# A two-stage FFT convolution with a soft mixture of experts: a first stage in tiles of 60 and 30 columns, x loaded two chunks at a time, and the last 26 rows of z loaded through GpSimd

## The chip, the cores and the metric

The kernel runs on one core of a Trainium2 chip. The metric is the device time of one execution in microseconds (us), the median of several runs. All data are float32. Engines are named as in the profile: PE is TensorE (PEld its weight loads), DVE is VectorE, ACT is ScalarE, POOL is GpSimd, SP is SyncE, which here only issues transfers.

## The reference

A causal long convolution of 8 sequences of 5696 tokens by 128 channels with one filter per channel, then a soft mixture of experts over all 45568 tokens: each of 32 slots (8 experts of 4) takes a softmax over tokens, each token a softmax over slots.

```python
# convolution: x (8, 5696, 128), h (5696, 128)
L = 2 * S
y = irfft(rfft(x, n=L, axis=1) * rfft(h, n=L, axis=0)[None], n=L, axis=1)[:, :S, :]
x = y.reshape(B * S, D)
# soft mixture of experts: phi (128, 32), w1 (8, 128, 1024), w2 (8, 1024, 128)
logits = x @ phi
d = softmax over tokens of logits          # columns
slot_input = (d.T @ x).reshape(E, 4, D)
slot_out[e] = maximum(slot_input[e] @ w1[e], 0) @ w2[e]
c = softmax over slots of logits           # rows
out = c @ slot_out
```

## The kernel before

The transform is split in two steps, 5696 = 89 x 64 with 90 frequencies in the first factor (`N1`) and 64 in the second (`N2`). Only half of a symmetric pair of columns is computed: a fold (sum and difference of a column and its mirror) halves the work. The filter h counts as group 0, the 8 sequences as groups 1 to 8. Each group has 8 chunks of 4 columns and their 4 mirrors; a chunk is one step `t` of the main loop.

- **First stage** (`load_x`, `fold`, `stage_a`). `load_x(c)` loads a chunk with its mirror columns into one of three buffers `xc`, in two DMAs on SP (80 rows and 9 rows, pieces of 2 KB). `fold` (L202, POOL) writes the sum (comp 0) or the difference (comp 1) into `x`. `stage_a(c, comp)` multiplies it by two 128-wide tables `s1` (L213: 128 rows, 128 columns, 512 moved), which hold the 90 frequencies in two blocks of 45 columns; ACT copies each bank to `fst` (L215), and two DMAs on SP store it in the DRAM scratch `f` (L219) in pieces of 1 KB. A fp32 product shows as two matmul records in the profile.
- **Second stage** (`load_g`, `stage_b1`, `stage_b2`), in units of 4 frequencies (the 12th unit of a group has 1). `gt` is loaded from `f` on SP (128 partitions, 4 KB each; L237), multiplied by `wt` (L251, 64x64 quarters) into the two-bank PSUM tile `bt`; DVE multiplies by the filter's spectrum (L269, L278) into `yf`; `stage_b2` transforms back with `vt` (L293) into the two-bank tile `bz`, ACT copies it to `zst` (L298), and SP stores it in the scratch `z` (L301).
- **Third stage** (`load_pair`, `stage_c1` to `stage_c6`), in pairs of chunks. `load_pair(T)` brings z into the one buffer `zc`: 64 of the 90 rows to partitions 32 to 95, and 26 rows in four DMAs of 8, 8, 8 and 2 rows to every fourth partition of 0 to 31 (`z_blocks`), 16 KB a row, all on SP (L329). `stage_c1` multiplies by `i1` (L348, two halves of 64 columns in one bank); ACT and DVE undo the fold (L353 to L361), and its second part `after` makes four sums on POOL (L367) that give the tokens `y`. Then come the transposes of y (c2, L376), the logits (c3, L385), the row maxima and exponentials (c4, L414 to L430; c5, L437; `softmax`, L445 to L450), the slot sums (`dispatch`, L461) and the token weights, kept in the scratch `c_t` (c6, L485).
- **Tail.** After the last first and second stages, the remaining five pairs of the third stage run by themselves with a second z buffer `zd`, whose unused rows are copied from `zc` as zeros (L656); then the experts (L761 to L791) and the output stage (L806 to L833), which writes 23 MB.

The order of the work is written out by hand: each engine, and each queue of DMA issues, runs its instructions in program order, and an instruction that waits holds up those behind it. The main loop (L561 to L645) runs step t: the z load of the coming pair, prefetch of `gt` for the next step, `load_x(t + 3)`, `stage_a(t, 0)`, `fold(t + 1, 0)`, dispatch, a second-stage unit, the third stage's products (every other step), transposes, a second-stage unit, `stage_a(t, 1)`, `fold(t + 1, 1)`, logits, and the rest. First-stage steps are t = 0 to 71, second-stage units t = 9 to 80, third-stage products start at t = 27. A step has one or two units of the second stage in turn.

Four PSUM banks (`bank()`) are shared in turn by all stages but the second, which has its own two two-bank tiles, `bt` and `bz`.

Of the kernel before, what the change touches and what calls it, by code (L numbers as in the profile page):

```python
# [17 lines left out]
def z_blocks(n):  # L18

    left = [(64 + 8 * j, min(8, n - 64 - 8 * j), j, 4) for j in range((n - 57) // 8)]  # L20
    return [(0, 64, 32, 1)] + left


def transform_tables(S, N1, N2, CH, X0, F0, F1):
# [20 lines left out]
    NP = N1 // 2  # L45
    part = s1
    s1 = np.zeros((P, 3, P))
    for a, p in enumerate((F0, F1)):
        s1[X0:X0 + R1, :, p:p + NP] = part[:, :, a * NP:(a + 1) * NP]
# [26 lines left out]
def kernel(  # L76
# [44 lines left out]
    X0, F0, F1 = 20, 6, 82  # L121
# [4 lines left out]
        for n, t in zip(("s1", "i1", "w", "v", "turn"), transform_tables(S, N1, N2, CH, X0, F0, F1))]  # L126
    fd = [nc.dram_tensor(f"f_{g}", (2, N2, NP, 2, D), F32, kind="Internal").ap() for g in range(B + 1)]
# [34 lines left out]
    s1 = apool.tile([P, 3, P], F32, name="s1", tag="s1", bufs=1)  # L162
# [12 lines left out]
    xf = [apool.tile([P, CH, D], F32, name=f"x{i}", tag=f"x{i}", bufs=1) for i in range(2)]  # L175
    xcs = [apool.tile([P, 2, CH, D], F32, name=f"xc{i}", tag=f"xc{i}", bufs=1) for i in range(3)]
# [3 lines left out]
    def load_x(c):  # L180
        if c >= (B + 1) * NJ:
            return
        g, j = divmod(c, NJ)
        src = (h if g == 0 else x[g - 1]).rearrange("(a n) d -> a n d", n=N2)
        t_ = xcs[c % len(xcs)]
        gap = N2 - CH * (2 * j + 1)
        for r in (slice(0, SPLIT), slice(SPLIT, R1)):
            v = src[r, CH * j:CH * (j + 1), :]
            v = bass.AP(tensor=v.tensor, offset=v.offset,
                        ap=[v.ap[0], [gap * D, 2], [1, CH * D]])  # L190
            nc.sync.dma_start(
                out=t_[X0 + r.start:X0 + r.stop, :, :, :].rearrange("p s n d -> p s (n d)"), in_=v)
        xs[c] = t_
# [3 lines left out]
    def fold(c, comp):  # L197
# [3 lines left out]
        y_ = xf[comp]  # L201
        nc.gpsimd.tensor_tensor(out=y_[:, :, :], in0=t_[:, 0, :, :], in1=t_[:, 1, ::-1, :],  # L202
# [3 lines left out]
    def stage_a(c, comp):  # L206
        g, j = divmod(c, NJ)
        src = folded.pop((c, comp))
        tab = (0, 1) if comp == 0 else (1, 2)
        st = apool.tile([P, CH, 2, D], F32, name="fst", tag="fst", bufs=5)  # L210
        for G in range(2):
            p = bank()
            nc.tensor.matmul(p[:, :], s1[:, tab[G], :],  # L213
                             src[:, :, :].rearrange("p n d -> p (n d)"), start=True, stop=True)
            nc.scalar.activation(st[:, :, G, :],  # L215
                                 p[:, :].rearrange("p (n d) -> p n d", d=D), AF.Copy)
        n0 = comp * HALF + CH * j
        for a, p in enumerate((F0, F1)):
            nc.sync.dma_start(  # L219
                out=fd[g][a, n0:n0 + CH, :, :, :].rearrange("n q c d -> q n (c d)"),  # L220
                in_=st[p:p + NP, :, :, :].rearrange("k n c d -> k n (c d)"))


# [7 lines left out]
    def load_g(u):  # L231
        if u >= (B + 1) * NW:
# [3 lines left out]
        t_ = bpool.tile([P, 4, 2, D], F32, name="gt", tag="gt", bufs=3)  # L236
        nc.sync.dma_start(  # L237
            out=t_[:, 0:n, :, :].rearrange("p q c d -> p (q c d)"),
            in_=fd[g].rearrange("a r q c d -> (a r) (q c d)")[:, 8 * w * D:(8 * w + 2 * n) * D])
        gs[u] = t_  # L240

    def stage_b1(u, share):
        g, w, us = parts(u)
        t_ = gs.pop(u)
        tag = "bz" if g == 0 and w % 2 else "bt"
# [15 lines left out]
        pi = bpool.tile([P, 4, 2, D], F32, name="p", tag="pi", bufs=2)  # L261
# [20 lines left out]
    def stage_b2(u):  # L282
# [5 lines left out]
        bz = bps.tile([P, 2, 2, 2 * D], F32, name="bz", tag="bz")  # L288
        for o, (i, n) in enumerate(us):
            for q in range(n):  # L290
                r = slice(q * HP, (q + 1) * HP)
                for a in range(2):
                    nc.tensor.matmul(bz[a * HP:(a + 1) * HP, q, o, :], vt[r, i, a, :],  # L293
# [4 lines left out]
        nc.scalar.activation(st[:, 0:m, 0:n, :].rearrange("p o q x -> p q o x"),  # L298
                             bz[:, 0:n, 0:m, :], AF.Copy)
# [8 lines left out]
    zn = used = None  # L308
# [12 lines left out]
    def load_pair(T):  # L321
# [3 lines left out]
        t_ = zring.pop(0)  # L325
        zring.append(t_)
        w_ = 2 * 2 * CH * 2 * D
        for r, n, p, step in z_blocks(N1):
            nc.sync.dma_start(  # L329
# [3 lines left out]
        zs[T] = t_  # L333

    def stage_c1(T, between):
        t_ = zs.pop(T)
        kr = used if t_ is zn else P
# [7 lines left out]
        def product(o, tab, q):  # L345
            p = bank()
            for h_ in range(2):
                nc.tensor.matmul(p[h_ * HP:(h_ + 1) * HP, :], i1[0:kr, tab, :],  # L348
                                 t_[0:kr, h_, o, :, q, :], start=True, stop=True)
# [200 lines left out]
    for c in range(1, 3):  # L550
        load_x(c)
# [7 lines left out]
    wait_b2 = []  # L559

    for t in range(last_front + 1):  # L561
# [12 lines left out]
        turns = {2: (1, 3), 1: (2,)}.get(len(us), ())  # L574

        def slot_b(place=None):
            if place is not None and place not in turns:
                return
# [8 lines left out]
        if pair(-1) is not None:  # L587
            load_pair(pair(-1))
        if t % NJ:
            prefetch(t + 1)  # L590
        if t < NA:
            load_x(t + 3)
            stage_a(t, 0)
            fold(t + 1, 0)
        if pair(3) is not None:
            dispatch(pair(3))
        if t < last_front:
            slot_b(1)
        T, U = pair(0), pair(2)
        if t == last_front:  # L600
            assert T is None and U is None
            slot_b()
# [9 lines left out]
        rows = (lambda: None) if U is None else (lambda: stage_c4(U))  # L612
        after = None
        if T is not None:
            after = stage_c1(T, rows)
        else:
            rows()
# [245 lines left out]
```

## Time and profile before

| | us |
|---|---|
| median of 3 runs (lowest, highest) | 899.32 (898.45, 901.66) |
| the profiled execution's own time | 901.4 |
| its span, first to last instruction | 899.6 |
| PE busy in the span | 808.7 (90%) |
| DVE busy | 645.0 (72%) |
| ACT busy | 480.9 (53%) |
| POOL busy | 405.8 (45%) |
| first-stage matmuls L213, 576 records | 274.6 |
| third-stage products L348, 480 records | 117.7 |
| folds L202 on POOL, 144 of 1276 ns | 183.6 |
| evacuations L215, 288 of 597 ns | 171.8 |
| evacuations L298, 96 of 972 ns | 93.3 |

The core moved 272.44 MB by DMA (mean 303 GB/s), nearly all issued by SP; nothing was issued by POOL. The packets of that queue took 90.1% of the span of the 16 DMA engines.

How to read it: a matmul's end is modelled in the profile, so a PE that is busy is not PE at its peak, and matmuls that run side by side on different columns of the array share their time. Durations are those of single instructions on their engine; the DMA share is the mean busy share of the 16 DMA engines. The chain of waits follows the work that ended last back to its beginning, and names at each step what released it.

### The profile page before, as it was taken

Reading aid. Unit: us, or ns where it says so; the run is one execution under the profiler, and the core shown is the slowest. Engines: PE = TensorE matmul, PEld = TensorE weight load, DVE = VectorE, ACT = ScalarE, POOL = GpSimd, SP = SyncE. Lnnn points to the kernel's source line nnn. Section 1 sums busy time; section 2 is a strip of 40 time slices with the busy share of each in tenths; the row PEclk is TensorE's granted clock in tenths of the full one; section 3 lists DMA queues with packets and bytes.
Section 4 is the critical chain, followed back from the end, with each engine's and each line's share of the span. In section 5 each row is a group of like instructions: output and inputs, shape, how many; then the busy total and the mean of one; then the engine's idle time right before and its main releaser. Section 6 shows DMA issues by size and latency. Waiting matters only on the chain.

```text
span 899.6 us, 19379 instructions
## 1 busy us (share of the span) xinstructions
PE 808.7 (90%) x7220; PEld 424.0 (47%) x7220; DVE 645.0 (72%) x928; ACT 480.9 (53%) x888; POOL 405.8 (45%) x385
## 2 busy tenths in 40 slices
PE   6969888799999999999999999999988777978893
PEld 2323344344445544455555445444444444444793
DVE  3049776668778888888888777888867886873542
ACT  3624445456655566665566666666644434673441
POOL 4624323345555555555555555555533343681000
PEclk9979999999999999999999999999988999987855
DMA  9989999999999999999999999999985887770898
GB/s 297 279 262 330 301 322 333 313 333 334 308 312 335 325 309 314 330 320 316 328 319 311 318 334 321 302 330 316 320 284 202 302 281 263 270 294 2 307 405 330
DMA packets 156967, 272.44 MB, mean 303 GB/s; under 512 B 12182, under 2 KB 114838, under 8 KB 153733
## 3 DMA queue, kind: packets, MB, share of 16 engines
q1 hardware_dynamic: 156299, 270.85, 90.1%
q8 instruction: 58, 0.95, 0.4%
q10 hardware_dynamic: 576, 0.36, 0.2%
q14 instruction: 34, 0.28, 0.1%
HBM read 142.86 MB, written 128.21 MB: 301 GB/s over the span
## 4 chain that ended last, share of the span: by engine, by line
PE 71%; DMA 18%; DVE 3%; issue 3%; ACT 2%; SPq 1%; POOL 0%; DVEq 0%; ACTq 0%
PE bank L213 24%; PE bank L348 12%; PE bt L251 10%; PE bz L293 8%; DMA gt<-f 5%; DMA out_dram<-o 5%; PE bank L376 5%; PE bank L461 3%; DMA zc<-z 3%; PE bank L385 2%; PE bank L437 2%; PE bank L414 2%; DMA xc<-in_x_dram 2%; DMA f<-fst 1%; PE bank L485 1%
## 5 line engine op out<-in xcount | busy, mean ns | idle before, releaser
L202 POOL TENSOR_TENSOR x<-xc 128x512 f32<-128x512 f32 x144 | 183.6, 1276 | 237.8 <-PE bank L213 188.4
L213 PE MATMUL bank<-x,s 128*128 128x512 f32 x576 | 274.6, 613 | 8.6 <-DMA xc<-in_h_dram 8.2
L215 ACT ACTIVATE fst<-bank 128x512 f32<-128x512 f32 x288 | 171.8, 597 | 91.4 <-PE bank L213 82.1
L298 ACT ACTIVATE zst<-bz 128x1024 f32<-128x1024 f32 x96 | 93.3, 972 | 196.0 <-PE bz L293 187.8
L269 DVE TENSOR_TENSOR p<-bt,Hi 128x1024 f32<-128x1024 f32 x96 | 113.0, 1177 | 105.0 <-PE bt L251 104.5
L213 PEld LDWEIGHTS bank<-x,s 128*128 128x128 f32 x576 | 102.2, 192 | 126.0 <-issue 95.6
L251 PE MATMUL bt<-gt,wt 64*64 64x256 f32 x1620 | 117.1, 396 | 37.5 <-DMA gt<-f 17.3
L348 PE MATMUL bank<-zc,i 128*64 128x512 f32 x480 | 117.7, 613 | 6.0 <-DMA zc<-z 4.3
L278 DVE TENSOR_TENSOR yf<-bt,p 128x512 f32<-128x512 f32 x192 | 119.4, 663 | 3.3
L269 DVE TENSOR_TENSOR bt<-bt,Hr 128x1024 f32<-128x1024 f32 x96 | 113.1, 1178 | 0.0
L251 PEld LDWEIGHTS bt<-gt,wt 64*64 64x64 f32 x1620 | 55.5, 134 | 114.1 <-issue 57.7
L293 PE MATMUL bz<-yf,vt 64*64 64x256 f32 x1440 | 104.7, 388 | 0.0
L367 POOL TENSOR_TENSOR y<-y,op 128x512 f32<-128x512 f32 x64 | 77.5, 1211 | 7.6 <-DVE op L353 4.9
L293 PEld LDWEIGHTS bz<-yf,vt 64*64 64x64 f32 x1440 | 61.7, 137 | 22.1 <-issue 0.9
L367 POOL TENSOR_TENSOR y<-y,om 128x512 f32<-128x512 f32 x54 | 64.0, 1185 | 2.1
L348 PEld LDWEIGHTS bank<-zc,i 128*64 128x64 f32 x480 | 30.1, 138 | 67.2 <-issue 46.4
L422 POOL MEMSET dt<- 64x8 f32 x32 | 3.4, 107 | 124.0 <-issue 65.4
L376 PE MATMUL bank<-ident,y 109*128 109x109 f32 x512 | 57.4, 267 | 0.7 <-DVE y L367 0.7
L376 PEld LDWEIGHTS bank<-ident,y 109*128 109x128 f32 x512 | 51.0, 146 | 13.5 <-POOL L L450 6.9
L378 ACT ACTIVATE yt<-bank 128x360 f32<-128x360 f32 x128 | 50.0, 481 | 0.9 <-PE bank L376 0.9
L816 PE MATMUL op<-so,cT 32*128 32x128 f32 x704 | 45.7, 382 | 5.2 <-ACT o L825 4.8
L269 DVE TENSOR_TENSOR p<-bt,turn 128x1024 f32<-128x1024 f32 (+1 forms) x12 | 14.1, 1173 | 49.9 <-PE bt L251 49.9
(97 smaller groups left out, 858.4 us busy)
## 6 DMA issues: line engine op xcount, KB each, us to landing
f<-fst SPq DMA_DIRECT2D x288, 180.0 KB
gt<-f SPq DMA_DIRECT2D x99, 512.0 KB
z<-zst SPq DMA_DIRECT2D x88, 512.0 KB
zc<-z SPq DMA_DIRECT2D x30, 1024.0 KB
xc<-in_x_dram SPq DMA_DIRECT2D x64, 320.0 KB
out_dram<-o SPq DMA_DIRECT2D x16, 1024.0 KB
zc<-z SPq DMA_DIRECT2D x90, 128.0 KB
out_dram<-o SPq DMA_DIRECT2D x8, 768.0 KB
```

The costliest lines, as they stand in the source:

```text
L202: nc.gpsimd.tensor_tensor(out=y_[:, :, :], in0=t_[:, 0, :, :], in1=t_[:, 1, ::-1, :], op=AL.subtract if comp else AL.add)
L213: nc.tensor.matmul(p[:, :], s1[:, tab[G], :], src[:, :, :].rearrange("p n d -> p (n d)"), start=True, stop=True)
L215: nc.scalar.activation(st[:, :, G, :], p[:, :].rearrange("p (n d) -> p n d", d=D), AF.Copy)
L251: nc.tensor.matmul(bt[q * HP:(q + 1) * HP, a, o, :], wt[r, 2 * i + q, :], t_[r, 2 * o + q, :, :].rearrange("p c d -> p (c d)"), start=True ...
L269: nc.vector.tensor_tensor(out=p_, in0=pv, in1=h_, op=AL.mult)
L278: eng.tensor_tensor(out=y_[r, 0:k, c, :], in0=pv[:, :, c, :], in1=pi[r, 0:k, 1 - c, :], op=op_)
L293: nc.tensor.matmul(bz[a * HP:(a + 1) * HP, q, o, :], vt[r, i, a, :], y_[r, a * m + o, :, :].rearrange("p c d -> p (c d)"), start=True, sto ...
L298: nc.scalar.activation(st[:, 0:m, 0:n, :].rearrange("p o q x -> p q o x"), bz[:, 0:n, 0:m, :], AF.Copy)
L348: nc.tensor.matmul(p[h_ * HP:(h_ + 1) * HP, :], i1[0:kr, tab, :], t_[0:kr, h_, o, :, q, :], start=True, stop=True)
L367: eng.tensor_tensor(out=part_, in0=part(v, 0), in1=o_[:, :, :], op=sign)
L376: nc.tensor.transpose(p[:, i * TR:(i + 1) * TR], ys[T][0:TR, k * CH + i, 0:D], ident[0:TR, 0:TR])
L378: nc.scalar.activation(yt[:, k * CH:(k + 1) * CH, :, :], of_tokens(p), AF.Copy)
```

## The change

The first stage's columns are regrouped. The 90 frequencies are interleaved, and the tables `s1` hold the first 60 in one 64-wide block and the last 30 in one 32-wide block. `first_low(c)` multiplies the sum and the difference of one chunk by the 64-wide block, two products into the two halves of one bank; `first_high(c)`, every second step, multiplies the sums and differences of two chunks by the 32-wide block, four products into the four quarters of one bank. The scratch `f` is laid out frequency by frequency, so that a partition's piece is stored as 4 KB and read back, by `load_g`, in pieces of 1 KB.

`load_x` loads two chunks at once (pieces of 4 KB) into one of two larger buffers, four steps ahead, on even steps alone. Both folds of a step are made together, into four buffers.

The 26 last rows of z come in four pieces of 8, 8, 5 and 5 rows, to every fourth partition of 0 to 31 and of 96 to 127 in turn, and these four DMAs are issued by POOL; the 64 rows remain SP's. In the tail the copy of zero rows becomes six copies, and the products on `zd` take 128 rows where they took 96.

The second stage's products use two two-bank tiles, `bt0` and `bt1`, in turn; its results go through the shared banks, one evacuation per bank. Buffer counts change (`gt` 3 to 4, `p` 2 to 1, `fst` 5 to 4). The loop's order is rewritten as two strings, one for odd steps (`ORDER_E`) and one for even steps (`ORDER_O`), in which the third stage's products stand on odd steps.

```diff
 def z_blocks(n):
-    left = [(64 + 8 * j, min(8, n - 64 - 8 * j), j, 4) for j in range((n - 57) // 8)]
+    left, r, j = [], 64, 0
+    while r < n:
+        m = min(8, (n - r + 1) // 2)
+        left += [(r, m, j, 4), (r + m, min(m, n - r - m), 96 + j, 4)]
+        r, j = r + 2 * m, j + 1
     return [(0, 64, 32, 1)] + left
...
-    fd = [nc.dram_tensor(f"f_{g}", (2, N2, NP, 2, D), F32, kind="Internal").ap() for g in range(B + 1)]
+    fd = [nc.dram_tensor(f"f_{g}", (NP, 2, N2, 2, D), F32, kind="Internal").ap() for g in range(B + 1)]
...
-    xf = [apool.tile([P, CH, D], F32, name=f"x{i}", tag=f"x{i}", bufs=1) for i in range(2)]
-    xcs = [apool.tile([P, 2, CH, D], F32, name=f"xc{i}", tag=f"xc{i}", bufs=1) for i in range(3)]
+    xf = [apool.tile([P, CH, D], F32, name=f"x{i}", tag=f"x{i}", bufs=1) for i in range(4)]
+    xcs = [apool.tile([P, 2, 2 * CH, D], F32, name=f"xc{i}", tag=f"xc{i}", bufs=1) for i in range(2)]
...
     def load_x(c):
-        if c >= (B + 1) * NJ:
+        if c % 2 or c >= (B + 1) * NJ:
             return
...
             v = bass.AP(tensor=v.tensor, offset=v.offset,
-                        ap=[v.ap[0], [gap * D, 2], [1, CH * D]])
+                        ap=[v.ap[0], [gap * D, 2], [1, 2 * CH * D]])
...
-    def stage_a(c, comp):
...
+    def first_stage(tiles, width):
+        st = apool.tile([P, CH, 2, D], F32, name="fst", tag="fst", bufs=4)
         for G in range(2):
             p = bank()
-            nc.tensor.matmul(p[:, :], s1[:, tab[G], :],
-                             src[:, :, :].rearrange("p n d -> p (n d)"), start=True, stop=True)
+            for o, (c, comp) in enumerate(tiles):
+                k = slice(0, HP) if width == HP else slice(HP, HP + QP)
+                nc.tensor.matmul(p[o * width:(o + 1) * width, :], s1[:, comp + G, k],
+                                 folded[(c, comp)][:, :, :].rearrange("p n d -> p (n d)"),
+                                 start=True, stop=True)
             nc.scalar.activation(st[:, :, G, :],
                                  p[:, :].rearrange("p (n d) -> p n d", d=D), AF.Copy)
+        for o, (c, comp) in enumerate(tiles):
+            g, j = divmod(c, NJ)
+            n0 = comp * HALF + CH * j
+            k0, n = (0, N1A) if width == HP else (N1A, N1 - N1A)
             nc.sync.dma_start(
+                out=fd[g].rearrange("q a r c d -> (q a) (r c d)")[k0:k0 + n, n0 * 2 * D:(n0 + CH) * 2 * D],
+                in_=st[o * width:o * width + n, :, :, :].rearrange("k n c d -> k (n c d)"))
+
+    def first_low(c):
+        first_stage([(c, comp) for comp in range(2)], HP)
+
+    def first_high(c):
+        both = [(c - 1 + i, comp) for i in range(2) for comp in range(2)]
+        first_stage(both, QP)
...
     def load_g(u):
...
-            out=t_[:, 0:n, :, :].rearrange("p q c d -> p (q c d)"),
-            in_=fd[g].rearrange("a r q c d -> (a r) (q c d)")[:, 8 * w * D:(8 * w + 2 * n) * D])
+            out=t_[:, 0:n, :, :].rearrange("p q c d -> p q (c d)"),
+            in_=fd[g][4 * w:4 * w + n, :, :, :, :].rearrange("q a r c d -> (a r) q (c d)"))
...
-        tag = "bz" if g == 0 and w % 2 else "bt"
+        tag = f"bt{u % 2}"
...
-        bz = bps.tile([P, 2, 2, 2 * D], F32, name="bz", tag="bz")
+        bz = [bank() for _ in range(us[0][1])]
...
-        nc.scalar.activation(st[:, 0:m, 0:n, :].rearrange("p o q x -> p q o x"),
-                             bz[:, 0:n, 0:m, :], AF.Copy)
+        for q in range(n):
+            nc.scalar.activation(st[:, 0:m, q, :],
+                                 bz[q][:, 0:m * 2 * D].rearrange("p (o x) -> p o x", o=m), AF.Copy)
...
-    def load_pair(T):
+    def load_pair(T, rest=None):
...
-        for r, n, p, step in z_blocks(N1):
-            nc.sync.dma_start(
+        for i_, (r, n, p, step) in enumerate(z_blocks(N1)):
+            if rest is not None and rest != (i_ > 0):
+                continue
+            (nc.gpsimd if i_ else nc.sync).dma_start(
...
+    ORDER_E, ORDER_O, XAHEAD = "XYf1wbV5s", "Xfz2b63dxPmb", 4
...
+        work_ = {
+            "z": lambda: load_pair(pair(-1), False) if pair(-1) is not None else None,
...
+            "V": lambda: load_pair(pair(-2), True) if pair(-2) is not None else None,
...
+            "x": lambda: load_x(t + XAHEAD) if t < NA else None,
...
+            "P": lambda: prefetch(t + 2),
...
+            "X": lambda: first_low(t) if t < NA else None,
+            "Y": lambda: first_high(t) if t < NA and t % 2 else None,
+            "f": lambda: [fold(t + 1, comp) for comp in range(2)] if t < NA else None,
+            "d": lambda: dispatch(pair(3)) if pair(3) is not None else None,
+            "b": lambda: slot_b(),
+            "1": lambda: after.append(stage_c1(T, lambda: stage_c4(U) if U is not None else None))
+            if T is not None else stage_c4(U) if U is not None else None,
+            "w": lambda: [a_() for a_ in after],
+            "2": lambda: stage_c2(pair(1)) if pair(1) is not None else None,
+            "6": lambda: stage_c6(pair(5)) if pair(5) is not None else None,
+            "5": lambda: stage_c5(U) if U is not None else None,
+            "3": lambda: stage_c3(pair(1)) if pair(1) is not None else None,
+            "m": lambda: column_max(pair(1)) if pair(1) is not None else None,
+            "s": lambda: softmax(U) if U is not None else None,
...
+        for c_ in (ORDER_E if t % 2 else ORDER_O):
+            work_[c_]()
...
-    held = slice(N1 // 64 * 8 + 3, used - 64, 4)
+    held = [slice(p + k + 4 * (n if k == 0 else 0), p - p % 32 + 32, 4)
+            for _, n, p, _ in z_blocks(N1)[3:] for k in range(3)]
...
-    nc.sync.dma_start(out=zn[held, :, :, :, :, :].rearrange("k h o n c d -> k (h o n c d)"),
-                      in_=zring[0][held, :, :, :, :, :].rearrange("k h o n c d -> k (h o n c d)"))
+    for v in held:
+        nc.sync.dma_start(out=zn[v, :, :, :, :, :].rearrange("k h o n c d -> k (h o n c d)"),
+                          in_=zring[0][v, :, :, :, :, :].rearrange("k h o n c d -> k (h o n c d)"))
```

## The prediction

> **What bounds the kernel now.** I began with the page's slices, to see whether one limit holds throughout.
>
> ```profile
> PE   6969888799999999999999999999988777978893
> ...
> DMA  9989999999999999999999999999985887770898
> GB/s 297 279 262 330 301 322 333 313 333 334 308 312 335 325 309 314 330 320 316 328 319 311 318 334 321 302 330 316 320 284 202 302 281 263 270 294 2 307 405 330
> ```
>
> One slice is 22.5 us. TensorE and the DMA engines both read 9 from the 8th to the 29th slice, so shares can't say which of them leads. Busy times by stretch come next (a line: start:end and length, then busy us and instructions of each engine, granted clock, DMA share, GB/s).
>
> ```profile
> 36.00:124.00 88.00, 72.87 (x432) 31.27 (x430) 56.87 (x65) 35.22 (x57) 35.02 (x28) 0.94 0.96 296
> 124.00:178.00 54.00, 44.23 (x352) 22.01 (x352) 36.24 (x42) 25.99 (x38) 16.53 (x13) 1.00 1.00 327
> ...
> 272.10:444.80 172.70, 172.70 (x1525) 86.09 (x1525) 141.51 (x203) 106.39 (x195) 96.90 (x90) 1.00 0.98 322
> ```
>
> Until 178 us (the fill, no third stage yet) TensorE has gaps (44 of 54 us busy) and the DMA engines have none: transfers bound it. From there to about 660 us (the steady stretch) TensorE has no gap, at a granted clock of 1.00, while the DMA share is 0.98. The chain of waits decides between them (start, us, what); this is one period, two chunks, 272.09 to 293.69 = 21.60 us:
>
> ```profile
> 272.09 3.44 PE bank L213 x8
> 275.52 1.03 PE bank L461 x32
> 276.55 1.02 PE bt L251 x16
> 277.57 0.86 PE bz L293 x16
> 278.44 1.64 PE bank L376 x16
> ...
> 280.54 1.81 PE bank L213 x4
> 282.35 0.74 PE bank L385 x8
> ...
> 284.98 1.92 PE bank L213 x4
> 286.90 1.87 PE bank L348 x8
> 288.76 0.59 PE bank L414 x4
> ...
> 293.69 3.44 PE bank L213 x8
> ```
>
> Only matmuls stand on it, and periods repeat at 21.60. So the steady stretch is TensorE's by the chain, with transfers close behind. 45 chunks of third-stage steps (27 to 71) make 22.5 such periods.
>
> **First stage.** A period now spends 3.44 + 1.81 + 1.92 = 7.17 us on 16 records of L213: 0.43 us per record of 512 columns (3.44 / 8). An fp32 product leaves two records. The change makes of a chunk's four 128-wide products two pairs 64 wide and, per two chunks, two fours 32 wide. Pairs of 64 are in the trace: L348's eight records last 1.87 us, four slots of 0.43 and 0.15 more, so two run side by side. Fours of 32 are L385's: 8 records of 360 columns in 0.74 us, two slots, so four run side by side. New: two low parts at 1.87 = 3.74; one high part of four slots, between 4 x 0.43 = 1.72 and L385's row scaled, 0.74 x 2 x 512/360 = 2.10. I take 1.85 (L385's excess over its slots, 0.74 - 2 x 0.30 = 0.14, added once). 3.74 + 1.85 = 5.59; saved 1.58 (1.33 to 1.71). Period: 20.02.
>
> **ScalarE and VectorE.** The first stage loses 2 evacuations of 0.597 per period; L298's 0.974 becomes two of 0.597, at 2.8 units: -1.19 + 0.62 = -0.57 us. ScalarE has 106.4 busy of 172.7, so this is nothing on the path. VectorE keeps its work, 141.5 / 8 = 17.7 us; in 20 us it is 88% busy, still covered. The second "bt" tile lets a new second-stage product start before VectorE has finished the last. Four shared banks now also take the second-stage results; each is refilled at least four fills later, with some 0.6 us of evacuation each: nothing.
>
> **The order.** After the last third-stage product TensorE now runs second stage 1.88, L437 0.59, first stage 1.87, then the transposes L376. Their input needs GpSimd's four sums:
>
> ```profile
> 353.20 1.94 PE L348 MATMUL bank<-zc,i 128*64 128x512 f32 x8
> ...
> 355.21 1.05 POOL L430 TENSOR_TENSOR L<-L,rm 128x512 f32<-128x512 f32 x1 [0.59 <-DVE rm L429]
> ...
> 356.21 2.45 POOL L367 TENSOR_TENSOR y<-y,op 128x512 f32<-128x512 f32 x2
> ```
>
> The products end at 355.14; the sums begin at 356.21 and take 2 x 2.45, ending 5.97 us after. The last quarter of L376 would start after 1.88 + 0.59 + 1.87 + 0.75 x 1.64 = 5.57: a stall of 0.40. Period: 20.42.
>
> **z on GpSimd.** Today all five pieces are SP's:
>
> ```profile
> L329 SPq DMA_DIRECT2D zc<-z x40: 544/602/1124, 275.4 to 427.8; - x40
> ```
>
> (min/median/max ns of one issue). Four of five move to GpSimd, behind the four sums and ahead of L450 (1.05) and of the next two folds (2 x 1.28, L202), and the next first stage waits for both folds. The products that read the old z ended 5.97 us before, so that wait costs nothing. Once in four periods the last piece also waits for the last z unit, whose result leaves PSUM some 4 us before; landings on the chain of waits took 3.9 to 4.2 us (f, at 38 to 47 us). I book 0, and up to 3 us in each of 5.6 such periods, 17 in all, for the range. From a period's start: 1.87 + 1.85 + 1.87 + 0.59 + 1.87 = 8.05, then 5.97, then 4s, 1.05 and 2.56: **17.63 + 4s**, s being one issue. No row shows a GpSimd issue. Below, 0.35 (SP's shortest for gt, 347 ns); above, 1.28, GpSimd's own longest common instruction. I take 0.60, the same transfer on SP: 20.0, just under 20.42. At 0.70 this chain takes over; at 1.28 it is 22.75. If the cover goes, the folds are late, then the first stage, then everything.
>
> The Trainium skill (DMA: Bandwidth & Descriptors, Specifications) puts the first byte at about 1 us from GpSimd and 0.6 from SP. No row here shows a GpSimd issue; if that difference were all GpSimd's own time, s would be an estimated 1.0 and the period 21.6, the gain gone.
>
> **Transfers.** Bytes stay: 322 GB/s x 21.6 us = 6.96 MB a period. First-stage results are written in 4 KB pieces instead of 1 KB and read back in 1 KB instead of 4 KB: one trades for the other. x comes in 4 KB instead of 2 KB, in two DMAs a period instead of four; SP loses 6 of some 24 issues, and SP isn't bound. x's load now waits for the second chunk's fold, with the gt loads queued behind it on SP; these have half a period or more before use. A period of 20.42 needs 341 GB/s. Bounds: 327 GB/s (124 to 178 us, share 1.00) gives 21.3 us; the output's 405 GB/s gives 17.2. I take the best slice of mixed traffic, 335: **20.78 us**, 0.82 saved, x 22.5 = **18.5 us**.
>
> On the z pieces the same page (Rules for kernel authors) speaks against the change: two transfers to disjoint partition halves share the same engines, and issuing from more queues gives no bandwidth. Another section (Why a DMA increments its semaphore by 16) has an SP transfer of 8 rows run on the lowest 8 engines, and GpSimd's start from a moving cursor, which would even the load. No row here splits the share by engine; by the first rule the period stays at 20.8 to 21.3, by the second TensorE's 20.4 is reached.
>
> **Fill and tail.** The fill (36 to 178 us) moves the same bytes at full DMA share; slices 4 to 8 spread from 301 to 333 GB/s, 5% about their middle, so I book 0, between -7 and +7 us. At the tail's start the one copy of zero rows becomes six: five more issues at 0.6, 3 us at most; 1 taken. A contraction over 128 rows instead of 96 changes no row (L348: 604 against 613 ns).
>
> **Sum.** Span 899.6 - 18.5 + 0 + 1 = 882.1; the profiled execution took 901.4, 1.8 around its span, so 883.9; it lies 2.1 above the median, 899.3, which becomes **881.8, say 882**.
>
> **Rivals.**
> *TensorE's rate is reached* (25%): the even z load and longer x bursts give 341 GB/s. For: the 405 GB/s. Against: no mixed slice above 335. 22.5 x 1.18 = 26.6, fill up to -7: 867 to 874; with the shortest high part (1.71 saved), 864.
> *Transfers take the bound* (17%): 327 GB/s holds, perhaps less as 1 KB reads replace 4 KB. For: share 1.00 at that rate. Against: the evener z. 22.5 x 0.3 = 6.8: 893; with the fill's +7, 900.
> *GpSimd's issue, the slower side* (14%): 17.63 + 4s passes 21.60 at s = 0.99. For: its in-order queue stands between third stage and next first stage. Against: 602 ns for the same issue on SP. At 1.28 it is 22.75: 22.5 x 1.15 = +26: 926; at 1.1, 910.
> *Fours of 32 don't run side by side* (2%): the high part then costs 3.4 and the gain is gone, about 900; L385's row speaks against.
> *The forecast* has 42%; its own range is 874 to 891, the fill's 7 us and the tail's 1 to 2 to either side.
>
> About 0.5%, 4.5 us, is what a measurement of this kernel can tell from no change. Faster by more: the forecast, the first rival and half of the second, 0.42 + 0.25 + 0.08 = 0.75. Within: most of the rest of the second and the fours, 0.09. Slower: 0.16, GpSimd and the second's worst end. The range reaches from below the first rival's middle, with a good fill, 860, to the mild end of the slow side, 904.
>
> **What would show it.** L213's busy time per period falls from 7.2 to 5.6 and its records come in fours; the chain's period reads 20.4 to 20.9. GpSimd issues at or under 0.7 us, and no first-stage matmul waits for L202. GB/s of 335 or more in the steady stretch; about 330 to 178 us. Wrong if the chain there names GpSimd or DMA, or if gt's landings stand on it past 200 us.

## The result, and the profile after

| | before | after |
|---|---|---|
| median (lowest to highest of 4 runs each, side by side), us | 900.49 (898.45 to 902.51) | 950.87 (949.67 to 956.66) |
| ratio, 95% interval | | 1.0572 (1.0521 to 1.0623) |
| span of the profiled execution, us | 899.6 | 947.9 |

The change makes the kernel slower by 5.7%. The forecast was 882 us, its range 860 to 904: wrong in sign.

The page of after, second part (40 slices, now of 23.7 us): most slices move less than before.

```profile
DMA  8888789999999999999999999999988886863698
GB/s 269 251 259 254 212 235 331 291 320 330 299 291 300 314 295 300 318 310 308 304 308 305 297 291 294 313 304 318 308 283 281 289 304 229 282 227 126 243 406 342
```

The same three stretches as in the prediction, after:

```profile
36.00:124.00 88.00, 59.15 (x396) 18.51 (x392) 42.22 (x48) 23.20 (x39) 34.46 (x28) 0.86 0.83 245
124.00:178.00 54.00, 38.24 (x400) 15.68 (x395) 33.93 (x37) 19.37 (x35) 14.80 (x12) 0.95 0.95 285
272.10:444.80 172.70, 158.54 (x1583) 74.35 (x1580) 126.56 (x192) 94.19 (x195) 109.56 (x119) 0.98 0.99 307
```

In the first stretch of the fill the DMA share has dropped from 0.96 to 0.83: something now keeps transfers from being issued. (The granted clock is lower there too, 0.86 against 0.94; TensorE is busy for 59 of the 88 us, and no run separates the clock's part.) In the steady stretch TensorE, which had no gap in 172.7 us, idles 14.

To split the loss by stage I take the first product of the third stage as the end of the fill. The view of the tile zc gives the first and last start of these products, before and then after:

```profile
L348 PE MATMUL bank<-zc,i x480: 592/592/1112, 179.0 to 792.1; 128*64 128x512 f32 x160
```

```profile
L374 PE MATMUL bank<-zc,i x480: 592/592/1061, 207.7 to 844.4; 128*64 128x512 f32 x160
```

The products of the pair 22 periods later start at 650.5 and 700.1. So the fill loses 28.7 us, the 22 periods 20.9 (471.5 to 492.4; 21.43 to 22.38 each), and the rest, 249.1 and 247.8, gains 1.3, which is less than this part differs among the runs below (241 to 255). Sum 48.3, the difference of the spans.

What one of these periods waits for stands in the timeline of after (start, us, engine, line; in brackets the idle time before):

```profile
489.29 2.52 POOL L212 TENSOR_TENSOR x<-xc 128x512 f32<-128x512 f32 x2
...
491.84 3.09 SPq L200 DMA_DIRECT2D xc<-in_x_dram  x2
...
494.98 2.29 SPq L259 DMA_DIRECT2D gt<-f  x3
...
499.73 1.94 PE L374 MATMUL bank<-zc,i 128*64 128x512 f32 x8
...
503.67 1.09 PE L273 MATMUL bt<-gt,wt 64*64 64x256 f32 x16 [2.00 <-DMA gt<-f]
```

Read it from below. TensorE is done with the third stage's products at 501.67 and waits 2.00 us for gt. SP issued that gt only at 494.98, because the x burst is ahead of it: its buffer came free with the fold's end at 491.81, and its two DMAs took SP 3.09 us. Then gt took 8.65 us to land (494.98 to 503.62 on the chain of waits). The next period has the same wait, 2.03 us. The view of TensorE's waits in the 22 periods (207.7 to 700.1 us; total, times, longest) says what they come to:

```profile
PE bt L273 <- DMA gt<-f: 36.0, 21, 2.3
PE bank L374 <- DMA zc<-z: 4.4, 7, 1.2
```

TensorE is busy for 447.4 of these 492.4 us, 20.34 a period, and 36.0 of the other 45.0 us are waits for gt.

In the fill the same place costs more:

```profile
45.41 7.21 SPq L232 DMA_DIRECT2D f<-fst  x8
...
54.12 1.73 SPq L259 DMA_DIRECT2D gt<-f  x3
...
55.94 11.23 SPq L232 DMA_DIRECT2D f<-fst  x8
...
61.07 1.98 PE L273 MATMUL bt<-gt,wt 64*64 64x256 f32 x16 [5.57 <-DMA gt<-f]
```

SP is held for 7 and 11 us by eight stores of f each, which wait for ScalarE's copies of first-stage results (L226; 34.7 us of SP's waits from 36 to 178 us are for these); x and gt stand behind them. Until its first third-stage product TensorE waits 37.5 us for gt, where before it was 15.7.

What was to be gained is there all the same, in the groups of the page of after:

```profile
L223 PE MATMUL bank<-x,s 128*32 128x512 f32 (+1 forms) x1152 | 226.8, 624 | 18.5 <-POOL x L212 17.5
...
L357 POOL DMA_DIRECT2D zc<-z x124 | 65.1, 531 | 22.8 <-DMA z<-zst 17.4
```

The first stage's busy time is 226.8 us where L213 had 274.6, and a z issue on GpSimd takes 0.53 us.

### The profile page after: what moved, and what is told of

The parts are those of the page before. It is cut to its first block, busy times and chain, and to the rows that moved or that the text cites. A ratio compares the mean times of both kernels' runs of the same rounds, so it can differ in the third digit from the quotient of the medians.

```text
span 947.9 us, 20381 instructions
## 1 busy us (share of the span) xinstructions
PE 783.2 (83%) x7796; PEld 385.6 (41%) x7796; DVE 625.7 (66%) x927; ACT 444.2 (47%) x904; POOL 469.9 (50%) x517
## 4 chain that ended last, share of the span: by engine, by line
DMA 30%; PE 26%; POOL 8%; DVE 6%; SPq 3%; issue 2%; ACT 2%; DVEq 0%; POOLq 0%; ACTq 0%
DMA gt<-f 17%; PE bank L223 5%; PE bt L273 4%; DMA out_dram<-o 4%; PE bank L315 4%; POOL y L393 3%; PE bank L402 3%; PE bank L374 3%; DMA zc<-z 3%; SPq L200 2%; POOL x L212 2%; DMA f<-fst 2%; DMA z<-zst 2%; DMA cl<-c_t 2%; DVE yf L300 1%
## 5 line engine op out<-in xcount | busy, mean ns | idle before, releaser
L223 PE MATMUL bank<-x,s 128*32 128x512 f32 (+1 forms) x1152 | 226.8, 624 | 18.5 <-POOL x L212 17.5
L321 ACT ACTIVATE zst<-bank 128x512 f32<-128x512 f32 (+1 forms) x184 | 98.6, 585 | 243.8 <-PE bank L315 226.6
L226 ACT ACTIVATE fst<-bank 128x512 f32<-128x512 f32 x216 | 127.9, 598 | 128.1 <-PE bank L223 108.8
L273 PE MATMUL bt<-gt,wt 64*64 64x256 f32 x1620 | 121.5, 410 | 73.9 <-DMA gt<-f 73.5
L315 PE MATMUL bank<-yf,vt 64*64 64x256 f32 x1440 | 104.5, 398 | 19.4 <-DVE yf L300 19.0
L223 PEld LDWEIGHTS bank<-x,s 128*32 128x32 f32 (+1 forms) x1152 | 56.2, 128 | 152.8 <-issue 79.3
L315 PEld LDWEIGHTS bank<-yf,vt 64*64 64x64 f32 x1440 | 58.0, 138 | 51.5 <-issue 30.5
L357 POOL DMA_DIRECT2D zc<-z x124 | 65.1, 531 | 22.8 <-DMA z<-zst 17.4
L402 PE MATMUL bank<-ident,y 109*128 109x109 f32 x512 | 62.3, 274 | 10.2 <-POOL y L393 9.5
L379 DVE TENSOR_TENSOR y<-bank,y 128x512 f32<-128x512 f32 x32 | 22.1, 690 | 62.9 <-PE bank L374 62.1
```

Of the source, the lines that this page charges most:

```text
L223: nc.tensor.matmul(p[o * width:(o + 1) * width, :], s1[:, comp + G, k], folded[(c, comp)][:, :, :].rearrange("p n d -> p (n d)"), start=Tr ...
L226: nc.scalar.activation(st[:, :, G, :], p[:, :].rearrange("p (n d) -> p n d", d=D), AF.Copy)
L273: nc.tensor.matmul(bt[q * HP:(q + 1) * HP, a, o, :], wt[r, 2 * i + q, :], t_[r, 2 * o + q, :, :].rearrange("p c d -> p (c d)"), start=True ...
L315: nc.tensor.matmul(bz[q][a * HP:(a + 1) * HP, o * 2 * D:(o + 1) * 2 * D], vt[r, i, a, :], y_[r, a * m + o, :, :].rearrange("p c d -> p (c ...
L321: nc.scalar.activation(st[:, 0:m, q, :], bz[q][:, 0:m * 2 * D].rearrange("p (o x) -> p o x", o=m), AF.Copy)
L357: (nc.gpsimd if i_ else nc.sync).dma_start(out=t_[p:p + (n - 1) * step + 1:step, :, :, :, :, :].rearrange("k h o n c d -> k (h o n c d)"), ...
```

## The experiments

Each stage of every run, read as above ("first" is the start of the first third-stage product, "22 periods" the time from there to the pair 22 later, both in one profiled execution of each run; ratios are to the kernel before, run beside it, with 95% intervals):

| run | median us | ratio (interval) | first | 22 periods |
|---|---|---|---|---|
| before | 900.5 | | 179.0 | 471.5 |
| after | 950.9 | 1.0572 (1.0521, 1.0623) | 207.7 | 492.4 |
| e1 f's layout alone | 897.6 | 1.0017 (0.9980, 1.0053) | 180.2 | 470.3 |
| e2 after, old layout of f | 984.6 | 1.0989 (1.0896, 1.1082) | 218.1 | 513.5 |
| e3 after, gt ahead of x | 931.6 | 1.0386 (1.0324, 1.0447) | 190.4 | 485.8 |
| e4 after, z on SP, same places | 1000.7 | 1.1129 (1.1030, 1.1229) | 212.1 | 538.6 |
| e5 before, x bursts alone | 905.2 | 1.0082 (1.0055, 1.0110) | 187.0 | 470.7 |
| e6 before, z's 26 rows on GpSimd | 923.4 | 1.0262 (1.0208, 1.0316) | 179.5 | 484.5 |
| e7 before, first stage alone | 962.5 | 1.0684 (1.0610, 1.0758) | 191.2 | 523.2 |
| e8 after, x by the chunk | 922.7 | 1.0260 (1.0189, 1.0331) | 187.5 | 481.5 |
| e9 e7, both folds early | 896.3 | 0.9994 (0.9958, 1.0029) | 188.2 | 460.2 |
| e10 e8, gt ahead, z on SP early | 911.4 | 1.0155 (1.0090, 1.0221) | 184.0 | 475.7 |
| e11 before, no mirror columns | 890.6 | 0.9945 (0.9912, 0.9978) | 175.6 | 468.6 |
| e12 e8, no mirror columns | 913.0 | 1.0173 (1.0127, 1.0220) | 179.1 | 473.9 |
| e13 e9, gt two steps ahead | 905.6 | 1.0085 (1.0052, 1.0119) | 182.4 | 470.4 |
| e14 e13, high part early | 898.2 | 0.9999 (0.9967, 1.0031) | 187.4 | 465.3 |
| e15 e8, gt ahead of x | 917.7 | 1.0226 (1.0180, 1.0271) | 188.4 | 477.2 |
| e16 e3, z on SP early | 907.7 | 1.0084 (1.0049, 1.0119) | 189.6 | 465.5 |
| e17 e3, SP's piece of z early | 931.4 | 1.0369 (1.0334, 1.0405) | 196.7 | 477.2 |
| e18 e16, z on SP late | 933.3 | 1.0396 (1.0359, 1.0433) | 190.8 | 489.6 |

The expectations name theories by letters: L is the layout of f (reads in 1 KB pieces), Q the order in SP's queue, G the z pieces issued by GpSimd, D a lower rate of the DMA engines when reads come in bunches, O waits in the order of issue.

### The layout of f (e1, e2)

```diff
 e1, on before
-    fd = (2, N2, NP, 2, D)     # stored in 1 KB pieces, read in 4 KB
+    fd = (NP, 2, N2, 2, D)     # stored in 4 KB pieces, read in 1 KB
 e2, on after: the reverse, a pair of chunks now stored in 12 DMAs instead of 8
```

> The kernel before with one part of the change alone: the scratch f laid out frequency by frequency, stored in 4 KB pieces and read back in 1 KB pieces. Theory L (the 1 KB reads of gt make the DMA engines the bound): slower by 30 to 60 us, 930 to 960, under 300 GB/s from 124 to 178 us. Theory Q (the layout is neutral; gt waits on SP behind the x burst, which waits for a fold): within 8 us of the kernel before, 892 to 908. Theory G (the z pieces from GpSimd): also within 8 us.

> The changed kernel with f's old layout: stored in 1 KB pieces by 12 instead of 8 DMAs per two chunks, read back in 4 KB pieces. Theory L: the loss goes and the first stage's gain shows, 870 to 900, gt landing in about 6 us instead of 9 to 10. Theories Q and G: 940 to 960, as the changed kernel.

e1 is no change: one size of piece does trade for the other. In e2 the old layout makes the loss larger, 984.6 us, which no theory had; it also puts four more issues per pair on SP. The layout isn't the cause. That the number of issues ahead of gt and z on SP is what costs in e2 would fit, but isn't tested by itself.

### gt behind x (e3)

```diff
-    ORDER_E, ORDER_O = "XYf1wbV5s", "Xfz2b63dxPmb"
+    ORDER_E, ORDER_O = "XYf1wbV5s", "Xfz2b63dPxmb"    # P loads gt, x loads x
```

> The changed kernel with the gt loads issued before the x burst in even steps. Theory Q: gt no longer waits for the fold, the steady period falls from 22.3 us towards 20.5, 905 to 925 in all. Theory L: the DMA engines stay at a share of 0.99 and the time within 10 us of 951. Theory G: likewise.

Two letters exchanged give 17.3 us back in the fill and 6.6 in the 22 periods; in all that is less than theory Q had (931.6 us against 905 to 925). The view of the tile gt, in the fill (36 to 178 us), has what TensorE and its weight loads waited for, added up; after, and e3:

```profile
  DMA gt<-f: 46.9, 11
```

```profile
  DMA gt<-f: 22.3, 11
```

Before, it was 24.4. In the steady stretch gt was 35.8% of the chain of waits in after (250 to 640 us) and is 2.7% in e3; in its place stands z, at 32.5%. In e3's 22 periods (190.4 to 676.3 us) TensorE waits for gt no more, and for z instead:

```profile
PE bank L374 <- DMA zc<-z: 19.8, 16, 1.8
```

The timeline of e3:

```profile
486.51 2.10 POOL L357 DMA_DIRECT2D zc<-z  x4
...
488.89 0.49 SPq L357 DMA_DIRECT2D zc<-z  x1
...
498.81 1.51 PE L374 MATMUL bank<-zc,i 128*64 128x512 f32 x6 [1.84 <-DMA zc<-z]
```

This is the second wait that lay under the first, a closed loop through the one buffer of z: the products of the pair before began at 476.44; GpSimd makes their sums until 486.5, then issues z; SP issues its piece at 488.89, behind two stores of f; it lands 9.78 us later, and the next products begin at 498.81. Once round is 22.37 us, and between 476.44 and 498.81 the chain of waits has these products, what leads from them to the sums, the sums, the last transposes, one second-stage unit and the landing.

### z, its engine and its place (e4, e6, e16, e17, e18)

```diff
 e4, on after; e6 puts the pieces of after and (nc.gpsimd if i_ else nc.sync) into before
-            (nc.gpsimd if i_ else nc.sync).dma_start(
+            nc.sync.dma_start(
 e16, on e3: all five pieces on SP, at "z", and that ahead of the low part
-    ORDER_E, ORDER_O = "XYf1wbV5s", "Xfz2b63dPxmb"
+    ORDER_E, ORDER_O = "XYf1wb5s", "zXf2b63dPxmb"
 e17, on e3: "zXf2b63dPxmb", the pieces on GpSimd left; e18, on e16: "Xfz2b63dPxmb"
```

> The changed kernel with all z pieces issued by SP instead of GpSimd, at the same places. Theory G: faster by 15 us or more, under 935. Theory L: within 10 us of 951. Theory Q: the same or slower, 950 to 965, since SP then waits for z rows with gt behind them.

> The kernel before with the z pieces alone: four pieces over both partition halves, issued by GpSimd at the place where SP issued them. Theory D: within 8 us of the kernel before, GpSimd's issues at 0.52 us each. Theory Q: SP is rid of four issues and their waits, the same or up to 8 us faster. Theory G (z through GpSimd costs): slower by 10 us or more.

> After with gt ahead of x and z loaded whole by SP at the start of the step before its product, x in one burst per pair as in the change. The other open corner of the square: 924 to 929 us if the burst is the larger cost, 914 to 921 if GpSimd's loads are. A sum with the run before it well off 1843 us means that the two are not separate costs.

> After with gt ahead of x, and SP's piece of z (the 64 rows) issued at the start of the even step, ahead of the low part's stores of f, as in the run with z whole on SP; the 26 rows stay on GpSimd. In the run with gt ahead alone (931.6 us) the chain waits for SP's piece: issued at 488.89, behind two stores of f, it lands 9.78 us later and the products wait 1.84 us for it. Theory place: the 24 us between that run and z whole on SP (907.7) come from this piece's place in SP's queue; then 905 to 915 us here. Theory GpSimd: they come from GpSimd's issue and queue; then 924 to 932.

> The other half: z whole on SP, but issued behind the low part's stores of f, where the change has SP's piece. Theory place: the products wait for z again, 924 to 935 us. Theory GpSimd: 905 to 915 us, as with z ahead of the stores (907.7).

e4, slower than any theory had it, speaks against GpSimd's issue as the cause, but not for SP: the four pieces now stand ahead of x and gt in SP's queue and hold it for 3.46 us (at 489.73), gt's landing stays first on the chain of waits (31% over 272 to 617 us), and a period is 24.5 us. In e6, in the order of before, GpSimd's pieces cost 0.6 us a period (21.43 to 22.02), 13 us in 22 periods. In these TensorE's third-stage products wait 8.7 us for z, where before it was 0.4, and 4.9 more that the profile puts to stores of f. e6's windows and the last line of its tile view of zc (272 to 617 us):

```profile
272.10:444.80 172.70, 168.35 (x1508) 84.83 (x1498) 136.33 (x195) 102.94 (x188) 111.32 (x119) 1.00 0.94 311
```

```profile
DMA to landing us min/median/max: 5.9/7.0/8.1
```

No bandwidth is won (311 GB/s for 322), and the pieces land 7.0 us after their issue, which is itself behind the sums in GpSimd's queue (sums from 493.15 to 498.01, then a fold and L452, z at 500.69, in one period). The rule that the prediction weighed, of the Trainium skill (DMA: Bandwidth & Descriptors, Rules for kernel authors), that issuing from more queues gives no bandwidth, holds here.

e16 then repairs the steady stretch: 465.5 us for 22 periods, 6.0 better than before. With e3's two letters and e16's place and engine of z, 43 of the 50 us that the change had cost are given back (907.7 us). Its windows:

```profile
272.10:444.80 172.70, 164.76 (x1678) 76.58 (x1670) 132.29 (x204) 98.83 (x202) 97.37 (x90) 1.00 0.98 323
```

The x bursts, the layout and the bytes are those of after, which moved 307 GB/s in the same stretch: neither bursts nor 1 KB reads hold the rate at 307, as theories D and L would have it. And gt lands in 5.2 to 6.2 us on e16's chain of waits (272 to 617 us), where after's took 8.7 to 10.7.

e16 differs from e3 in two things, and e17 and e18 undo one each. Both theories fall: neither the place alone (e17, 931.4 us) nor the engine alone (e18, 933.3 us) gives back the 24 us between e3 and e16. In e17 SP's piece is ahead of the stores of f, by 0.6 us here, and the products still wait, for GpSimd's last piece, which lands at 499.14; in e18 they wait for five pieces on SP behind the stores. Timelines of e17 and e18:

```profile
487.24 2.10 POOL L357 DMA_DIRECT2D zc<-z  x4
487.94 0.49 SPq L357 DMA_DIRECT2D zc<-z  x1
...
499.38 1.08 PE L374 MATMUL bank<-zc,i 128*64 128x512 f32 x4 [1.70 <-DMA zc<-z]
```

```profile
490.85 4.55 SPq L357 DMA_DIRECT2D zc<-z  x5
...
502.69 1.51 PE L374 MATMUL bank<-zc,i 128*64 128x512 f32 x6 [3.27 <-DMA zc<-z]
```

The products need all five pieces. With one of them late, behind GpSimd's sums or behind f's stores, it helps little that the others are early. In the 22 periods e17 does gain 8.6 us over e3, and its fill loses 6.3; why its fill is longer stays open.

### x in bursts (e5, e8, e10, e15)

```diff
 e5, on before, at the end of even steps; e8, on after, the reverse: every step, but with 4 buffers and load_x(t + 4)
-    xcs: 3 x [P, 2, CH, D],  load_x(t + 3) every step
+    xcs: 2 x [P, 2, 2 * CH, D],  load_x(t + 4) every second step;  fst 5 -> 4 in e5
 e10: e8 with "XYf1wbx5s", "zXf2b63dPxmb" and z whole on SP
 e15: e8 with "XYf1wbVx5s", "Xfz2b63dPxmb"
```

> The kernel before with the x bursts alone: two chunks per load, issued at the end of even steps, with one fst buffer less for room. Theory D (reads that come in bunches lose rate on the DMA engines, whoever issues them): slower by 8 to 25 us, x pieces taking longer per byte. Theory Q (only the order on SP costs, where gt waits behind a burst that waits for a fold): within 6 us of the kernel before, since here gt is not behind such a wait in every step.

> The changed kernel with x loaded by the chunk, one load in every step, into four buffers that are free a step earlier. Theory D: the bunch is split, 905 to 925, pieces of 2 KB at less engine time per byte. Theory Q: no wait for the fold ahead of gt, 925 to 935 as with gt first. Neither: within 8 us of 951.

> The changed kernel with x by the chunk, gt ahead of x, and all of z issued by SP at one place at the start of even steps, GpSimd issuing nothing. Theory O (waits in the issue queues are the loss): 890 to 910. Theory D: the DMA share at 0.98 and about the time of e8, 915 to 930, as long as a read of z or x takes as long as there.

> After with gt ahead of x and x by the chunk; the rest of z stays on GpSimd. It closes a square: x in bursts or by the chunk, z on GpSimd or whole on SP, gt ahead of x in all four. Bursts with GpSimd took 931.6 us, chunks with SP 911.4. If the two costs are separate ones that add, this run and the next together make 1843 us; if the burst is the larger one this run is at 914 to 919 and the next at 924 to 929; if GpSimd's loads are the larger one, this run is at 922 to 929 and the next at 914 to 921.

In before, bursts and the one fst buffer less cost 8.0 us in the fill and nothing in the steady stretch; e5 doesn't separate the two. In after bursts cost 28 us (950.9 to 922.7): there gt stands behind them. With gt ahead (e3, e15, e16, e10) bursts still cost 13.9 us with z on GpSimd, and with z on SP they cost nothing that is clear of the noise (907.7 against 911.4, intervals that overlap): 907.7 + 917.7 = 1825 against 931.6 + 911.4 = 1843, so these are not costs that add. That would fit a burst that also delays z; no run tests it.

### The first stage (e7, e9, e13, e14)

```diff
 e7, on before: stage_a(t, 0) -> first_low(t); stage_a(t, 1) -> first_high(t) in odd steps; layout of f; folds at their places; fst 5 -> 4
 e9, on e7
             first_low(t)
-            fold(t + 1, 0)
+            for comp in range(2):
+                fold(t + 1, comp)
...
-            fold(t + 1, 1)      # this one stood behind GpSimd's four sums
 e13, on e9: gt bufs 3 -> 4, p bufs 2 -> 1, prefetch(t + 2) at most places where it was t + 1
 e14, on e13: first_high(t) directly behind first_low(t); x buffers 6 -> 4, fst 4 -> 5
```

> The kernel before with the first stage in 60 and 30 columns alone (with the layout of f that goes with it, and folds into six buffers), all else in its old order, x loaded by the chunk, z by SP. Theories D and Q both: the saving of 1.6 us a period shows as far as the DMA engines give it, 870 to 890. If it stays at 897 to 903, the DMA engines are the bound at the old period already and no saving on TensorE can show.

> The first stage alone in the old order, as e7, but both folds of a step stand right after the low part, ahead of GpSimd's four sums. Theory O (e7 lost because the new first stage needs both folds at once, and the second came behind the sums): the first-stage matmuls no longer wait for GpSimd, under 915, and at best 880 to 895. Theory D (the transfers are the bound): the DMA share returns to 0.97 or more and the time stays at 895 to 915. If it stays above 945, the matmuls of 60 and 30 columns cost something that the busy times don't show.

> The order of before with the new first stage and both folds early (the run at 896.3 us), and now gt loaded two steps ahead: gt in four buffers, p in one, the same bytes of memory. If what is left of the fill's loss (first c1 product at 188.2 us against 179.0) is gt landing late, the first product comes at 179 to 183 us and the kernel at 887 to 891. If it is the first stage's own chain (two parts, four buffers of fst, stores that hold SP), the first product stays above 186 us and the kernel at 893 to 899. The steady period stays at 20.8 to 21.0 us either way.

> As the run with gt two steps ahead, but with the high part directly behind the low part and ahead of the folds in odd steps: four folded buffers do instead of six, and the room gives fst a fifth buffer. If ACT's wait for f's landing and the fst buffers hold the fill, the first product comes 2 to 5 us earlier than in that run. If the folds behind the high part (3.8 us later in every second step) cost TensorE, the steady period rises from 20.9 to 21.1 to 21.4 us and the kernel is 4 to 11 us longer than it.

The groups of the steady stretch (272 to 617 us), e7 and e9:

```profile
L217 PE MATMUL bank<-x,s 128*64 128x512 f32 (+1 forms) x454 | 103.5, 627 | 32.2 <-POOL x L206 32.2
```

```profile
L217 PE MATMUL bank<-x,s 128*64 128x512 f32 (+1 forms) x538 | 96.0, 601 | 0.0
```

e7's 962.5 us is far outside both of its expectations. The new low part wants both folds at once; left behind the sums, the second costs 2.9 us a period (23.78 to 20.92). With both early, e9 has the shortest periods of all runs: 20.92 in the mean, single ones from 20.0, the forecast's period of TensorE, to 22.3. Its windows:

```profile
272.10:444.80 172.70, 163.16 (x1673) 76.59 (x1670) 136.25 (x209) 98.70 (x182) 94.87 (x89) 1.00 0.97 327
```

That is 327 GB/s at a share of 0.97, near the forecast's bound by transfers (20.78 at 335). But TensorE's waits don't show transfers as the bound. In the 22 periods (188.2 to 648.3 us) it is busy for 435.3 us, 19.78 a period, and waits 11.9 for ScalarE's copies of the transposes, against 5.2 for z and 3.8 for gt:

```profile
PE bank L401 <- ACT yt L394: 11.9, 22, 1.0
PE bank L364 <- DMA zc<-z: 5.2, 5, 2.1
```

The 11.4 us won in the 22 periods are mostly given back by the fill, 9.2, and no difference to before can be measured (0.9994).

e13 answers one question and opens another. With gt two steps ahead the fill ends at 182.4: loading gt earlier gives back 5.8 of e9's 9.2 us. But the periods rise to 21.38 and the gain is gone. e14 has 21.15 and a fill of 187.4, although gt's waits in the fill fall further (24.4 us before, 25.9 in e9, 19.9 in e13, 12.2 in e14): the time waited for gt doesn't give the length of the fill by itself, and what else lengthens it, the folds behind the high part perhaps, isn't shown. No version that computes the whole result beats before by a measurable amount.

### Fewer bytes (e11, e12)

e11 and e12 leave out the mirror columns of x and h, so what they compute is no longer the convolution; they only ask what fewer bytes are worth.

```diff
-                        ap=[v.ap[0], [gap * D, 2], [1, CH * D]])
+                        ap=[v.ap[0], [gap * D, 1], [1, CH * D]])    # no mirror columns
```

> The kernel before with the mirror columns of x and h not loaded (they stay zero): 5% fewer bytes by DMA in the steady stretch, nothing else changed. If TensorE bounds the steady stretch of before, its period stays at 21.6 us and only the fill gets shorter, 880 to 895 in all. If the transfers bound it, the period falls to 20.5 to 21, under 875.

> As e8 (the changed kernel, x by the chunk), with the mirror columns of x and h not loaded: 5% fewer bytes. Theory D (its steady stretch is the transfers'): 5% of the fill and the steady stretch go, 25 to 40 us less than e8, 883 to 898. Theory O (waits in order and latency): at most 15 us less than e8, 908 to 923.

5% fewer bytes change before's period little (21.43 to 21.30): TensorE bounds it, as the chain said. e8's falls from 21.89 to 21.54 and its DMA share to 0.91, yet it doesn't reach 20.4: landing times and order hold it, not bandwidth alone (TensorE still waits 12.0 us for z from 272 to 617 us).

## Why the prediction was wrong

Its steps, in its order.

- **First stage: right.** "3.74 + 1.85 = 5.59" a period. The chain of waits of after has 3.72 for a low and a high part together (8 and 16 records) and 1.87 for the other low part: 5.59. Fours of 32 columns run side by side.

```profile
472.44 3.72 PE bank L223 x24
...
529.95 1.87 PE bank L223 x8
```

- **GpSimd's issue: right in kind, 0.60 booked, 0.53 measured.** The rival built on it (slow from 0.99) got the sign of the result by luck: its mechanism isn't what made the kernel slow.
- **The order of gt: the step that failed.** The prediction put it: "x's load now waits for the second chunk's fold, with the gt loads queued behind it on SP; these have half a period or more before use". That is 10.2 us. From gt's issue to where TensorE wants it there are 6.7 us (494.98 to 501.67), because x's wait and its 3.09 us of issue come off first, and gt needs 8.65 to land. Price: 36.0 us of waiting in 22 periods, booked as nothing. e3 shows the order as the cause: the waits for gt are gone there. In the fill that gives time back; in the steady stretch the next wait, for z, takes most of the place.
- **z's landing: the second half of the same mistake.** "The products that read the old z ended 5.97 us before, so that wait costs nothing" looked at when GpSimd may issue and not at when the data land. The landing was taken from two rows of f, 3.9 and 4.2 us, at 38 to 47 us. The chain of waits of before had z's own landings, at about twice that:

```profile
190.58 8.44 DMA zc<-z
234.51 7.26 DMA zc<-z
```

At 4 us the loop of e3 would be an estimated 22.37 - 9.78 + 4 = 16.6 us and harmless; at 9.78 it is what the products wait for.
- **Fill: booked 0, between -7 and +7; measured +28.7.** Same bytes do not mean same time: the DMA share fell to 0.83 while SP's issues wait. The prediction took the share of 0.96 for "transfers bound it"; the chain of waits of before, from 36 to 179 us, has first-stage products at 26.3% and gt's landings at 24.9%, in turn, so that a later issue of gt can cost time there. gt behind x is 17.3 of the 28.7 (e3). The remaining 11.4 are near e9's 9.2, which comes with the first stage and both folds early, and near the 8.5 and 9.4 of e8 and e15, with x by the chunk; e13 gives 5.8 of e9's back by loading gt earlier. That these parts add up isn't shown.
- **Transfers: near in the number, not shown in kind.** 335 GB/s taken, 327 reached in e9, whose period of 20.92 is near the 20.78 booked; but TensorE's longest wait there is for ScalarE, so the nearness is partly luck. 307 in after is no ceiling of its transfers, as e16's 323 shows; why the DMA engines read 0.99 busy at 307 isn't shown.
- **Tail: +1 booked, -1.3 measured**, within what it differs between runs.
- **Two readings.** TensorE's digits are 9 from the ninth slice on, not the eighth. And the periods of before don't all repeat at 21.60: in the steady stretch they go between 21.60 and 21.16, with 21.43 in the mean of 22, so there was a little less to save.

In the forecast's own terms, as spans: 882.1 was added up. The periods took 20.9 more where 18.5 were to be saved, 39.4; the fill 28.7; the tail 2.3 less than booked. That is 947.9, the span measured, as it must be; it shows that the loss lies in the waits of the periods and in the fill, both booked as nothing. The prediction had named the sign that would tell: wrong "if gt's landings stand on it past 200 us". It gave that no price and no chance.

What stays open: what the part of the fill's loss is that remains with gt ahead of x, why gt and z land later in after and e3 than in e16, and which order would keep e9's period and e13's fill together.

## What to carry to other kernels

When a load is moved behind another in an issue queue, work out three times: when the one ahead may start, how long its issues hold the queue, and how long the landing of *that* tile took in *that* stretch; the slack is what is left. A single-buffered tile makes a loop of last read, work ahead of the issue, issue and landing, and a load in several pieces is as late as its last piece. A saving on the engine that has no gap shows only until the next wait: of the 1.18 us a period that the forecast gave TensorE (21.60 to 20.42), e9 shows 0.5, with TensorE busy for 19.78 of 20.92 us. And a DMA share near 1 doesn't say that transfers bound a stretch; the chain of waits does.

## What the runs showed of the hardware

- The same landing takes quite different times, and the DMA share doesn't tell which. On the chains of waits gt took 4.3 to 5.6 us in e9's fill (at 45, 85 and 98 us) and 8.2 there at 137 us; between 272 and 617 us it took 5.2 to 6.2 in e16 (share 0.98, 323 GB/s) and 8.7 to 10.7 in after (0.99, 307 GB/s); z took 8.9 to 10.4 there in e3 and 4.8 to 7.0 in e16.
- SP's issue varies too: a store of f is 0.39 us at its median in the fill of after and up to 3.17; two loads of x, 1.35 us in after's fill (at 43.83), take 3.09 in its steady stretch (at 491.84).
- GpSimd's issue of 5 or 8 rows of 16 KB is steady, 0.52 us at the least and 0.57 at the most in the steady stretch, and GpSimd is held for that time.
- Four fp32 products on 32 columns each run side by side: the 16 records of a high part last 3.72 - 1.87 = 1.85 us, four slots of 0.43 and 0.13 more.
